# Talking-heads attention and gated layers on one core: score rows issued ahead of the stores of x in each slot

## The chip, the cores and the metric

One core of a Trainium2 chip. The metric is the device time of the kernel in microseconds (us), a median over runs; a profile of one execution by the hardware profiler goes with it.

## What is computed

```python
scores = (q @ k.T) / sqrt(64)                        # 4 batches, 12 heads, 448 x 448
scores = einsum('bhij,hg->bgij', scores, w_pre)      # heads mixed before the softmax
attn = softmax(scores)                               # exp(scores - max) / (sum + 1e-9)
attn = einsum('bhij,hg->bgij', attn, w_post)         # and after it
x = (attn @ v) as 1792 rows of 768
out = (sigmoid(x @ w_gate) * (x @ w_val)) @ w_out    # d_ff 1536
```

All inputs and the output are float32.

## The kernel before

The kernel has two stages in one program: the attention (`_attention`), which writes x to a buffer in device memory called xs, and the gated layers (`_Moe`), which read xs. The instruction order on every engine is fixed by the program's order; each engine works through its own queue, and semaphores hold an instruction until what it reads is there and what it overwrites has been read.

**Blocks and units.** Each batch has 448 query rows, cut into blocks of 120, 120, 120 and 88. A block is worked on in units: one or two sets of 10 query rows for all 12 heads. There are 16 blocks and 92 units (6, 6, 6 and 5 per batch; each batch's last unit has one set).

**Slots.** The loop that the diff touches (line 404 on) goes through slots `s`. In one slot several units are at different steps. The ones that matter here:

- `rows_until(s + LEAD, ...)` calls `regroup(s + 6)` (line 197): two transfers on SyncE's queue, one for each x in 0 and 1, that gather the score rows of unit s + 6 from the block's score tile `st` into a tile `T` with heads on the partitions. There are four `T` tiles, so the one for unit s + 6 is free when the premix of unit s + 2 has read it.
- `premix(s + 3)` (line 207): TensorE mixes the heads of unit s + 3, reading `T` half by half and writing `pm` banks. Three `pm` banks serve two sets a unit, so each premix needs a bank that the exponential of the unit before must have read.
- `rowmax` (line 215, VectorE), `expo` (line 225, ScalarE), `norm`, `scale` (GpSimd), `p_lo` (VectorE), `postmix` (line 255, TensorE), `mix` (line 263, ScalarE): the softmax and the second mixing.
- `scores` (line 159) and `keep` (line 165): scores of a later block, into `st`.
- `av` (line 273): attn @ v of a finished block, two pairs of heads at a time. After the fourth and the sixth pair ScalarE copies the result into the tile `xt` (line 292), and a store of `xt` to xs is put on the list `stores`. There is one `xt` tile (`xp` has one buffer), so the next copy into it must wait until the store before has landed. `av` stands in the last part of a slot.
- `flush()` (line 269) issues what is on the list, on SyncE's queue (line 271). The list also holds, twice, a small transfer of a bound (`max_x`).
- Last in a slot come loads on SyncE's queue: v (line 172), k (line 137), q (line 145) for the batches and blocks to come, and raw weights of the gated layers (line 1037).

So SyncE's queue gets, slot by slot: the stores that the slot before has put on the list, the rows of unit s + 6, then the slot's loads. Each block's two stores are flushed in the fourth and the sixth slot after that of the block's last unit, and with them go the rows of unit s + 6. From slot 83 on (`s >= NU - LEAD - 3`) the rows of the next slot are already issued inside the slot, so that the call at the top of the loop finds nothing to do.

```python
    def flush():
        while stores:
            nc.sync.dma_start(out=stores[0][0], in_=stores.pop(0)[1])
```

Of the kernel before, what the change touches and what calls it, by code (L numbers as in the profile page):

```python
# [41 lines left out]
def _attention(ctx, tc, ins, B, H, S, D, xs, raws, make_moe):  # L42
# [37 lines left out]
    def qk_banks():  # L80
        return [ps_qk.tile([128, 512], F32, tag="qk", name="qk") for _ in range(2)]
# [71 lines left out]
    def scores(bi, c, sc):  # L153
        b, n = blocks[bi][0], R * blocks[bi][4]
        q, k = q_t[bi], k_t[b, c]
        for s0, s1 in ((0, 64), (64, max(n, 100))):
            for e in range(2):
                rows = slice(64 * e, 64 * e + 64)
                nc.tensor.matmul(sc[e][s0:s1, :S], lhsT=q[c][rows, s0:s1], rhs=k[rows, :], start=True, stop=True)  # L159

    def keep(bi, c, e, sc):
        n = R * blocks[bi][4]
        if c == e == 0:
            st_t[bi] = stg[bi % ST].tile([QB, H, S], F32, tag="st", name="st")
        (nc.vector.tensor_copy if e else nc.scalar.copy)(st_t[bi][:n, 2 * c + e], sc[e][:n, :S])  # L165
# [31 lines left out]
    def regroup(u):  # L197
        bi, r0s, _, _, i = units[u]
        sets, st, T = blocks[bi][4], st_t[bi], t_bufs[u % len(t_bufs)]
        at = 64 - HK  # L200
        for x in range(2):
            if len(r0s) == 2:
                nc.sync.dma_start(out=T[at:at + 2 * HK, x], in_=st[i + x:sets * R:sets])
            else:
                nc.sync.dma_start(out=T[at:at + HK, x], in_=st[i + sets * HALF * x:sets * HALF * (x + 1):sets])

    def premix(u):
        T = t_bufs[u % len(t_bufs)]
        banks = units[u][2]
        for x in range(2):  # L210
            for i, bank in enumerate(banks):
                rows = slice(64, 64 + HK) if i else slice(0, 64)
                nc.tensor.matmul(pm[bank][64 * x:64 * x + 64, :S], lhsT=w1[rows], rhs=T[rows, x], start=True, stop=True)  # L213

    def rowmax(u):
        nm = sm.tile([128, 2], F32, tag="nm", name="nm")
        for i, bank in enumerate(units[u][2]):
            nc.vector.tensor_reduce(nm[:, i:i + 1], pm[bank][:, :S], axis=AX.X, op=ALU.max, negate=True)  # L218
        nm_t[u] = nm

    def expo(u, i):
        if i == 0:
            e_t[u] = ep.tile([128, 2, S], F32, tag="e", name="e")
            ss_t[u] = sm.tile([128, 2], F32, tag="ss", name="ss")
        nc.scalar.activation(out=e_t[u][:, i], in_=pm[units[u][2][i]][:, :S], func=AF.Exp, bias=nm_t[u][:, i:i + 1],  # L225
                             scale=1.0, accum_out=ss_t[u][:, i:i + 1])

    def norm(u):
        ss = ss_t[u][:, :len(units[u][1])]
        nc.gpsimd.tensor_scalar(ss, ss, 1e-9, 1.0 / P_UP, op0=ALU.add, op1=ALU.mult)  # L230
        nc.vector.reciprocal(ss, ss)  # L231

    def scale(u):

        ph = pp.tile([128, 2, S], F16, tag="ph", name="ph")
        for i in range(len(units[u][1])):
            nc.gpsimd.tensor_scalar(ph[:, i], e_t[u][:, i], ss_t[u][:, i:i + 1], 1.0, op0=ALU.mult, op1=ALU.mult)  # L237
        p_t[u] = [ph]

    def p_lo(u):  # L240
        pl = pp.tile([128, 2, S], F16, tag="pl", name="pl")
        for i in range(len(units[u][1])):
            nc.vector.scalar_tensor_tensor(pl[:, i], e_t[u][:, i], ss_t[u][:, i:i + 1], p_t[u][0][:, i],  # L243
                                           op0=ALU.mult, op1=ALU.subtract)
        p_t[u].append(pl)

    def postmix(u):
        mx = two_banks(ps_mx, "mx").rearrange("p x (i c) -> p x i c", i=2)[:, :, :, :4 * HK]
        ph, pl = p_t.pop(u)
        for i in range(len(units[u][1])):  # L250
            for jb in range(4):
                for k, (p, w) in enumerate(((ph, w2hi), (ph, w2lo), (pl, w2hi))):
                    for x in range(2):
                        rows = slice(64 * x, 64 * x + 64)
                        nc.tensor.matmul(mx[:, x, i, jb * HK:(jb + 1) * HK], lhsT=p[rows, i, JB[jb]:JB[jb] + 128], rhs=w[rows],  # L255
                                         start=(k == 0), stop=(k == 2))
        mx = mx.rearrange("p x i c -> p (x i) c") if len(units[u][1]) == 2 else mx[:, :, 0]
        mx_t[u] = mx.rearrange("p y (g r) -> p y g r", r=HALF)

    def mix(u):  # L260
        bi, r0s = units[u][:2]
        out = mixes[bi % 2].rearrange("p j h s -> p (j h) s")[:, :, r0s[0]:r0s[-1] + R]
        nc.scalar.activation(out=out.rearrange("p g (y r) -> p y g r", r=HALF), in_=mx_t.pop(u), func=AF.Copy,  # L263
                             scale=1.0 / (P_UP * W_UP))
# [4 lines left out]
# [3 lines that stand above are left out]
# [26 lines left out]
    LEAD = 6  # L298
# [12 lines left out]
    for b in range(B):  # L311
# [3 lines left out]
        s = f + 5  # L315
        for i in range(H // 2):
            s = max(s + 1, f + 6 + 2 * (2 * i // QUAD))
# [79 lines left out]
    def rows_until(u, done):  # L397
        while done < min(NU, u + 1):
            regroup(done)
            done += 1  # L400
        return done

    next_dma = 0
    for s in range(min(min(plan), -LEAD), max(plan) + 1):
        flush()
        next_dma = rows_until(s + LEAD, next_dma)
        todo = plan.get(s, ())
        jobs = [args for fn, args in todo if fn is scores]
        ahead_u = [(s + SOFT, i) for i in range(len(units[s + SOFT][1]))] if 0 <= s + SOFT < NU else []
        if 0 <= s + 1 < NU:  # L410
            norm(s + 1)
            scale(s + 1)
        if ahead_u:
            premix(s + SOFT)
            rowmax(s + SOFT)

        def job(bi, c):
            sc = qk_banks()
            scores(bi, c, sc)
            return lambda e: keep(bi, c, e, sc)  # L420

        kept = job(*jobs[0]) if jobs else None
        for i, e in enumerate(ahead_u[:1]):
            expo(*e)
        if kept:
            kept(0)
            kept(1)
        for c in hooks.get(s, ()):
            c.close()
        if 0 <= s + 1 < NU:  # L430
            p_lo(s + 1)
        tail = (av, moe.between, moe.early)
        if s == NU - 1:
            nc.scalar.activation(out=iw, in_=sw, func=AF.Sigmoid)
        if 0 <= s < NU:
            postmix(s)
        elif s >= NU:
            moe.slot(NG + s - NU)
        if 0 <= s < NU:
            mix(s)  # L440
        for e in ahead_u[1:]:
            expo(*e)
        for fn, args in todo:
            if fn is not scores and fn not in tail:
                fn(*args)
        if s >= NU - LEAD - 3:
            next_dma = rows_until(s + 1 + LEAD, next_dma)
        if 0 <= s < NU:
            for i in range(len(units[s][1])):
                moe.slot(units[s][3] + i)  # L450
        for fn, args in todo:
            if fn in tail:
                fn(*args)
        for args in jobs[1:]:
            kept = job(*args)
            kept(0)
            kept(1)
# [751 lines left out]
@with_exitstack  # L1209
def kernel(ctx, tc, B, H, S, D, ins, out):  # L1210
    nc = tc.nc
    top = ctx.enter_context(tc.tile_pool(name="top", bufs=1))
    dram = ctx.enter_context(tc.tile_pool(name="dram", bufs=1, space=DRAM))
    xs = dram.tile([B, H * D // 128, 128, S], F32, name="xs")
    with tc.manual_schedule():
        raws = top.tile([128, 13 * H * D // 2], F32, name="raws")
        with ExitStack() as c2:
            moe = _attention(c2, tc, ins, B, H, S, D, xs, raws,
                             lambda NG: _Moe(tc, xs, ins, out, raws, NG, top))
        moe.run()  # L1220
# [72 lines left out]
```

## Time and profile before

| what | value |
|---|---|
| median of 3 runs | 790.5 us (789.5 to 790.78) |
| the profiled execution | 792.71 us, of which the span of its instructions is 790.9 us |
| TensorE busy (PE) | 765.7 us, 97% of the span |
| VectorE (DVE), ScalarE (ACT), GpSimd (POOL) busy | 631.6, 566.5 and 256.0 us |
| granted TensorE clock, mean | 0.995 |
| DMA, mean | 210 GB/s |
| a pair of transfers of score rows T<-st | 2 x 210 KB |
| a store xs<-xt | 240 KB (four pairs of heads), 120 KB (two) |

The span runs from the first to the last instruction. Busy shares count an engine's own work, without its waits and without the issuing of DMAs. SyncE has no work of its own: it issues transfers, and an entry of its queue that waits holds all that stand behind it. In a row of the timeline, the time in brackets is what the engine stood idle before the instruction, and behind the arrow what ended that wait, as far as the profile infers it; where a wait has several causes, the one named is the one that came last by the profile.

### The profile page before, as it was taken

How to read it: one execution, taken by the hardware profiler on the slowest of the kernel's cores; microseconds unless marked ns; L12 is line 12 of the kernel's file. 1: busy time of each engine (PE TensorE's matmuls, PEld its weight loads, DVE VectorE, ACT ScalarE, POOL GpSimd, SP SyncE). 2: the span in 40 equal slices, each digit the busy share in tenths (PEclk: the TensorE clock that was granted, in tenths of full speed). 3: DMA queues.
4: the chain of work that ended last, by engine and by line, in shares of the span. 5: the costliest groups of instructions: out<-in, count | busy, mean ns of one | idle time of the engine just before them, and what ended most of it. 6: DMA issues, size and time to landing. Idle time of an engine off the chain costs nothing.

```text
span 790.9 us, 23630 instructions
## 1 busy us (share of the span) xinstructions
PE 765.7 (97%) x9626; PEld 422.9 (53%) x9626; DVE 631.6 (80%) x1092; ACT 566.5 (72%) x1122; POOL 256.0 (32%) x426
## 2 busy tenths in 40 slices
PE   8999999899989999978999999999999999999998
PEld 2465665566656666554555455555555555555554
DVE  4998899699969898889996988679786999997111
ACT  3899899798989899786975877677856784563000
POOL 1563547354644455420312222224322221010000
PEclk9999999999999999999999999999999999999999
DMA  5787678747885474828506384664567788995001
GB/s 193 248 241 222 205 247 259 241 165 234 269 257 186 172 239 158 279 82 283 183 6 221 107 271 159 264 221 148 208 190 264 275 310 298 386 363 206 36 36 70
DMA packets 80716, 166.16 MB, mean 210 GB/s; under 512 B 20448, under 2 KB 57664, under 8 KB 80608
## 3 DMA queue, kind: packets, MB, share of 16 engines
q1 hardware_dynamic: 72304, 132.88, 50.8%
q0 software_dynamic: 7728, 31.27, 10.2%
q8 instruction: 75, 1.23, 0.6%
q10 hardware_dynamic: 576, 0.51, 0.2%
q14 instruction: 33, 0.27, 0.1%
HBM read 87.77 MB, written 38.15 MB: 159 GB/s over the span
## 4 chain that ended last, share of the span: by engine, by line
PE 83%; DVE 6%; ACT 5%; DMA 3%; issue 2%; POOL 1%; SPq 0%; DVEq 0%; ACTq 0%; POOLq 0%
PE bank L1147 30%; PE bank L1158 18%; PE pm L213 10%; PE qk L159 9%; PE av L282 8%; PE mx L255 7%; DVE m L1131 2%; ACT e L225 1%; ACT m L1126 1%; ACT mix L263 1%; DVE pl L243 1%; DMA T<-st 1%; DVE m L1140 1%; DMA max_w<-junk 1%; DMA k<-in_kp_dram 1%
## 5 line engine op out<-in xcount | busy, mean ns | idle before, releaser
L1147 PEld LDWEIGHTS <-m 128*128 128x128 f16 x1512 | 147.5, 98 | 143.3 <-DVE m L1131 4.1
L1147 PE MATMUL bank<-m,m 128*128 128x448 f16 x1116 | 214.7, 352 | 4.3 <-DVE m L1131 3.2
L237 POOL TENSOR_SCALAR ph<-e,ss 128x448 f16<-128x448 f32 x180 | 112.6, 638 | 151.6 <-DVE ss L231 108.7
L225 ACT ACTIVATE e<-pm,nm 128x448 f32<-128x448 f32 x180 | 115.4, 641 | 30.6 <-DVE nm L218 28.2
L218 DVE TENSOR_REDUCE nm<-pm 128x1 f32<-128x448 f32 x180 | 103.4, 615 | 31.7 <-PE pm L213 28.4
L243 DVE SCALAR_TENSOR_TENSOR pl<-e,ss,ph 128x448 f16<-128x448 f32 x180 | 115.8, 683 | 2.0 <-POOL ph L237 2.0
L213 PE MATMUL pm<-T,w 64*64 64x448 f32 (+1 forms) x720 | 109.7, 563 | 4.1 <-ACT raws L1078 3.5
L1158 PEld LDWEIGHTS <-m 128*128 128x128 f16 x756 | 74.0, 98 | 69.0
L159 PE MATMUL qk<-k,q 64*64 64x448 f32 x736 | 103.4, 545 | 2.8 <-ACT st L165 2.0
L263 ACT ACTIVATE mix<-mx 128x960 f32<-128x960 f32 (+1 forms) x92 | 104.5, 1136 | 1.4 <-PE mx L255 1.4
L255 PEld LDWEIGHTS <-ph 64*128 64x128 f16 x2880 | 63.4, 93 | 71.7 <-issue 42.3
L1158 PE MATMUL bank<-m,m 128*128 128x448 f16 x468 | 92.9, 352 | 0.0
L282 PE MATMUL av<-mix,v 128*64 128x120 f32 (+1 forms) x1504 | 83.8, 264 | 0.2 <-issue 0.2
L255 PE MATMUL mx<-w2hi,ph 64*128 64x60 f16 x1440 | 71.1, 189 | 7.6 <-ACT mix L263 5.2
L1147 PE MATMUL bank<-m 128*128 128x448 f16 x396 | 77.9, 352 | 0.0
L282 PEld LDWEIGHTS av<-mix,v 128*64 128x64 f32 x1504 | 73.6, 138 | 3.0 <-issue 0.8
L255 PE MATMUL mx<-w2lo,ph 64*128 64x60 f16 x1440 | 70.3, 188 | 1.0 <-issue 1.0
L255 PE MATMUL mx<-w2hi,pl 64*128 64x60 f16 x1440 | 70.1, 188 | 0.5 <-DVE pl L243 0.5
L1084 POOL CAST raws<-raws 128x768 f16<-128x768 bf16 x28 | 31.4, 1122 | 118.1 <-ACT raws L1078 118.1
L1078 ACT ACTIVATE raws<-raws 128x768 int16<-128x768 int8 (+1 forms) x72 | 60.2, 836 | 11.3 <-POOL raws L1084 11.1
L165 DVE COPY st<-qk 120x448 f32<-120x448 f32 (+1 forms) x92 | 56.6, 615 | 8.7 <-PE qk L159 8.7
L255 PEld LDWEIGHTS <-pl 64*128 64x128 f16 x1440 | 61.3, 93 | 1.7 <-issue 1.1
(127 smaller groups left out, 1043.1 us busy)
## 6 DMA issues: line engine op xcount, KB each, us to landing
T<-st SPq DMA_DIRECT2D x176, 210.0 KB
m<-w SPq DMA_DIRECT2D x60, 384.0 KB
raws<-in_w_dram SPq DMA_DIRECT2D x28, 767.6 KB
hs<-m POOLq DMA_DIRECT2D x48, 224.0 KB, 3.1
m<-hs SPq DMA_DIRECT2D x15, 672.0 KB
w<-m POOLq DMA_DIRECT2D x21, 384.0 KB, 4.4
w<-raws POOLq DMA_DIRECT2D x20, 384.0 KB, 4.7
v<-in_vb_dram SPq DMA_DIRECT2D x12, 512.0 KB
```

The costliest lines, as they stand in the source:

```text
L159: nc.tensor.matmul(sc[e][s0:s1, :S], lhsT=q[c][rows, s0:s1], rhs=k[rows, :], start=True, stop=True)
L213: nc.tensor.matmul(pm[bank][64 * x:64 * x + 64, :S], lhsT=w1[rows], rhs=T[rows, x], start=True, stop=True)
L218: nc.vector.tensor_reduce(nm[:, i:i + 1], pm[bank][:, :S], axis=AX.X, op=ALU.max, negate=True)
L225: nc.scalar.activation(out=e_t[u][:, i], in_=pm[units[u][2][i]][:, :S], func=AF.Exp, bias=nm_t[u][:, i:i + 1], scale=1.0, accum_out=ss_t[u ...
L237: nc.gpsimd.tensor_scalar(ph[:, i], e_t[u][:, i], ss_t[u][:, i:i + 1], 1.0, op0=ALU.mult, op1=ALU.mult)
L243: nc.vector.scalar_tensor_tensor(pl[:, i], e_t[u][:, i], ss_t[u][:, i:i + 1], p_t[u][0][:, i], op0=ALU.mult, op1=ALU.subtract)
L255: nc.tensor.matmul(mx[:, x, i, jb * HK:(jb + 1) * HK], lhsT=p[rows, i, JB[jb]:JB[jb] + 128], rhs=w[rows], start=(k == 0), stop=(k == 2))
L263: nc.scalar.activation(out=out.rearrange("p g (y r) -> p y g r", r=HALF), in_=mx_t.pop(u), func=AF.Copy, scale=1.0 / (P_UP * W_UP))
L282: nc.tensor.matmul(av_t[bi][64 * i:64 * i + 64, c % 4, :n], lhsT=vt[b, u][:, h + i, jb, :], rhs=mixes[bi % 2][:, jb, 2 * c + i, :n], start ...
L1078: self.nc.scalar.activation(out=out, in_=src, func=AF.Copy, scale=by)
L1147: self.nc.tensor.matmul(self.f32(bank), lhsT=w[a][:, k], rhs=x[b][:, k], start=self.START[i] and k == r == 0, stop=k == self.KH - 1 and r ...
L1158: self.nc.tensor.matmul(self.f32(bank), lhsT=w[a][:, k], rhs=b[bb], start=self.START[i] and j == k == r == 0, stop=j == OUT_TILES - 1 and ...
```

## The change

In each slot, the transfers of score rows are issued first and the stores on the list behind them; before it was the other way round.

```diff
--- before.py
+++ after.py
@@ -402,8 +402,8 @@
 
     next_dma = 0
     for s in range(min(min(plan), -LEAD), max(plan) + 1):
+        next_dma = rows_until(s + LEAD, next_dma)
         flush()
-        next_dma = rows_until(s + LEAD, next_dma)
         todo = plan.get(s, ())
         jobs = [args for fn, args in todo if fn is scores]
         ahead_u = [(s + SOFT, i) for i in range(len(units[s + SOFT][1]))] if 0 <= s + SOFT < NU else []
```

The instructions on TensorE, VectorE, ScalarE and GpSimd keep their order; only SyncE's queue differs. First place: SyncE at slot 9, the first store of the first block (`xs<-xt`), the rows of unit 15 (tile `T_173`, two transfers) and the loads around them. Before:

```order
L145 DMA q<-in_qp_dram 128x720
L1037 DMA raws<-in_w_dram 128x1536
L271 DMA xs<-xt 128x4x120
L203 DMA T_173<-st 120x1x448 x2
L137 DMA k<-in_kp_dram 128x448
L1037 DMA raws<-in_w_dram 128x1533
```

and with the change:

```order
L145 DMA q<-in_qp_dram 128x720
L1037 DMA raws<-in_w_dram 128x1536
L203 DMA T_173<-st 120x1x448 x2
L271 DMA xs<-xt 128x4x120
L137 DMA k<-in_kp_dram 128x448
L1037 DMA raws<-in_w_dram 128x1533
```

The store has moved behind the pair of rows; the load of k that follows is the same. The first stores of the blocks in slots 32 and 55 stand in the same way behind the rows of units 38 and 61.

Second place: SyncE at slots 26 to 29, where the loads of batch 2 begin. Before:

```order
L271 DMA xs<-xt 128x4x88
L203 DMA T_170<-st 120x1x448 x2
L203 DMA T_171<-st 120x1x448 x2
L172 DMA v<-in_vb_dram 128x1024
L271 DMA xs<-xt 128x2x88
L203 DMA T_172<-st 120x1x448 x2
L1037 DMA raws<-in_w_dram 128x1536
L203 DMA T_173<-st 120x1x448 x2
L172 DMA v<-in_vb_dram 128x1024
L137 DMA k<-in_kp_dram 128x448 x2
```

and with the change:

```order
L203 DMA T_170<-st 120x1x448 x2
L271 DMA xs<-xt 128x4x88
L203 DMA T_171<-st 120x1x448 x2
L172 DMA v<-in_vb_dram 128x1024
L203 DMA T_172<-st 120x1x448 x2
L271 DMA xs<-xt 128x2x88
L1037 DMA raws<-in_w_dram 128x1536
L203 DMA T_173<-st 120x1x448 x2
L172 DMA v<-in_vb_dram 128x1024
L137 DMA k<-in_kp_dram 128x448 x2
```

The raw weights, and the loads of v and k after them, now stand directly behind the store, and no longer behind the store and a pair of rows. In all, 26 stores of x move in this way.

## Rows read from the trace of the kernel before

**Rows 1.** The page, section 4: the chain that ended last, by engine.

```profile
PE 83%; DVE 6%; ACT 5%; DMA 3%; issue 2%; POOL 1%; SPq 0%; DVEq 0%; ACTq 0%; POOLq 0%
```

**Rows 2.** Windows: us, busy time (instructions) by engine, granted clock, DMA share, GB/s.

```profile
50.00:62.00 12.00, 12.00 (x307) 7.93 (x305) 9.93 (x21) 12.00 (x33) 7.95 (x12) 1.00 0.90 251
...
122.00:146.00 24.00, 21.44 (x476) 12.72 (x469) 19.74 (x42) 19.31 (x47) 15.08 (x21) 1.00 0.84 261
...
182.00:204.00 22.00, 22.00 (x502) 13.65 (x504) 21.02 (x53) 20.51 (x51) 10.32 (x21) 1.00 0.80 248
204.00:230.00 26.00, 23.99 (x543) 14.72 (x539) 22.52 (x48) 22.87 (x57) 17.68 (x24) 0.99 0.89 268
...
17.00:340.00 323.00, 311.67 (x7030) 187.54 (x7024) 282.21 (x605) 285.69 (x666) 161.30 (x280) 0.99 0.71 226
...
228.60:232.00 3.40, 3.40 (x16) 1.37 (x16) 0.92 (x4) 3.13 (x8) 1.44 (x3) 0.66 0.71 235
232.00:236.00 4.00, 4.00 (x92) 2.73 (x92) 2.68 (x6) 3.43 (x8) 0.00 (x0) 0.86 0.68 228
```

**Rows 3.** Waits on SyncE's queue: us in total, times, longest.

```profile
SPq L271 <- ACT xt L292: 65.1, 26, 10.6
```

**Rows 4.** Tile T: issues (ns min/median/max); waits ended by its landing (us, times).

```profile
L203 SPq DMA_DIRECT2D T<-st x176: 760/768/1335, 12.0 to 319.5; - x176
...
  DMA T<-st: 1.7, 4
```

**Rows 5.** Timeline of SyncE, slot 9: start, us, line, operation [idle before].

```profile
54.71 0.57 SPq L271 DMA_DIRECT2D xs<-xt  x1
```

**Rows 6.** Timeline of all engines, 60 to 70 us.

```profile
61.00 0.51 ACT L292 ACTIVATE xt<-av,sw 128x240 f32<-128x240 f32 x1
...
62.81 0.20 PEld L213 LDWEIGHTS pm<-T,w 64*64 64x64 f32 x4 [0.45 <-DMA T<-st]
...
68.74 0.22 PEld L159 LDWEIGHTS qk<-k,q 64*64 64x64 f32 x8 [0.77 <-ACT st L165]
...
69.55 0.64 ACT L225 ACTIVATE e<-pm,nm 128x448 f32<-128x448 f32 x1 [0.86 <-DVE nm L218]
```

**Rows 7.** Timeline of SyncE, 117 to 140 us.

```profile
120.18 0.38 SPq L271 DMA_DIRECT2D xs<-xt  x1
120.66 1.68 SPq L203 DMA_DIRECT2D T<-st  x2
122.42 0.45 SPq L1037 DMA_DIRECT2D raws<-in_w_dram  x1
...
137.09 0.38 SPq L271 DMA_DIRECT2D xs<-xt  x1
```

**Rows 8.** Timelines of ScalarE and TensorE's weight loads, 134 to 147 us.

```profile
136.16 0.14 PEld L213 LDWEIGHTS pm<-T,w 64*64 64x64 f32 x2 [0.75 <-DMA T<-st]
...
144.79 0.46 ACT L292 ACTIVATE xt<-av,sw 128x240 f32<-128x240 f32 x1 [3.56 <-DMA xs<-xt]
...
145.75 0.19 PEld L213 LDWEIGHTS pm<-T,w 64*64 64x64 f32 x2 [2.49 <-ACT raws L1078]
146.35 0.28 PEld L213 LDWEIGHTS pm<-T,w 60*64 60x64 f32 x6 [0.41 <-ACT e L225]
```

**Rows 9.** Timelines of SyncE, ScalarE and TensorE's weight loads, 219 to 231 us.

```profile
219.71 0.38 SPq L271 DMA_DIRECT2D xs<-xt  x1
...
222.11 1.63 PEld L282 LDWEIGHTS av<-mix,v 128*64 128x64 f32 x32
...
227.60 0.46 ACT L292 ACTIVATE xt<-av,sw 128x240 f32<-128x240 f32 x1 [1.79 <-PE mx L255]
...
228.57 0.19 PEld L213 LDWEIGHTS pm<-T,w 64*64 64x64 f32 x2 [1.14 <-ACT raws L1078]
229.16 0.19 PEld L213 LDWEIGHTS pm<-T,w 60*64 60x64 f32 x2 [0.40 <-ACT e L225]
229.65 0.29 PEld L213 LDWEIGHTS pm<-T,w 64*64 64x64 f32 x4 [0.30 <-DMA T<-st]
```

## The prediction

> **What bounds the kernel now.** I read the page first. The chain that ended last is TensorE for 83% [rows 1], so a transfer matters only where TensorE waits for it, directly or through another engine. The diff changes the order on SyncE's queue and nothing else, and only in the attention, so the second view is the busy time by stretch: from 17 to 340 us TensorE is busy 311.67 of 323.00 us [rows 2]. At most 11.3 us are to be had there, and whatever is added to its waits lasts to the end, because the gating layers begin from the x that the attention stores.
>
> Third come SyncE's own waits. In 26 places the store of x stands at the head of the queue until ScalarE has written xt, 65.1 us in all [rows 3]; the transfers of score rows, behind it, stand with it. Against that, TensorE waited for rows of T only four times, 1.7 us together, and one transfer of rows takes SyncE 0.768 us to issue [rows 4], a pair 1.68 [rows 7]. The obvious gain of the change, rows that come earlier, is therefore worth at most 1.7 us. The reader should keep this: the queue is held for long, but what it holds has slack.
>
> The timeline shows where there is no slack. The key and query loads of the next batch fall in three stretches, and in each the first store of a block is followed at once by a unit's rows.
>
> - **Slot 9** (A): store 54.71, its rows next. ScalarE writes the next xt at 61.00 without having waited; TensorE gets the second half of those rows at 62.81 [rows 5, 6].
> - **Slot 32** (B): store 137.09, its rows next in the queue [rows 7]. ScalarE stands still for 3.56 us until 144.79, when that store has landed (there is one xt tile, so the next copy into it waits for the store before): 7.7 us from issue to landing. TensorE stands for 2.49 us until 145.75 [rows 8].
> - **Slot 55** (C): store 219.71, its rows next. ScalarE stands until 227.60. The row names a postmix matmul, but xt reads av, whose weights were loaded from 222.11 on for 1.63 us; so it was the store again, 7.9 us after its issue. TensorE takes the first rows at 228.57, waits for ScalarE's exponentials at 229.16 and for the second rows at 229.65 [rows 9].
>
> The DMA engines are 0.90, 0.84 and 0.89 busy in these stretches, against 0.71 over the attention [rows 2].
>
> **The change, part by part.** No instruction is added or removed.
>
> *The push.* A store now lies behind two transfers of rows. Where the queue is backlogged, it should land about when those rows landed before. C: 229.65 − 227.60 = 2.05 us later. B: the last rows come into use in the weight loads at 146.35, so 146.35 − 144.79 = 1.56, say 1.6. A: 62.81 − 61.00 = 1.8, if the store landed just before 61.00. No row shows that landing; but successive transfers land 1.08 us apart at C (228.57 and 229.65), and 62.81 less twice that is 60.7, so I take nearly all of it, 1.75. The lower bound is 0 at A, and 0 at B and C if the DMA engines do not keep the order of issue.
>
> What hangs on it: ScalarE's xt copy, and behind it on ScalarE the exponential of the next unit, for which TensorE's premix needs its bank.
>
> - A: ScalarE shows no idle time from 61.00 until 69.55, and at 68.74 TensorE waits 0.77 us for a copy out of that train [rows 6]. So the whole delay reaches TensorE: **+1.75**.
> - B: premix's wait for ScalarE and its last rows fall into one row, 146.35, so TensorE loses about what ScalarE loses: **+1.6** before the next item.
> - C: the wait for ScalarE moves from 229.16 to 231.2 against 229.65 for the rows: +1.55, or +2.05 counted on ScalarE.
>
> *The lead.* The rows no longer stand behind the store that waits, so what follows the store is issued earlier by a pair's time: the raw weights at 122.42 could follow the store of 120.18 at about 120.66, 1.76 us earlier [rows 7], and the loads of batch 2 behind them likewise. Where the DMA engines had time free before, that lead is kept until B. I take 1.35 of 1.76, because the next unit's rows also need scores that are copied only in that slot: B is **+0.25**. Before A there is no earlier store, hence no lead. Before C the engines were already 0.80 busy from 182 to 204 [rows 2], where a transfer issued earlier mostly queues longer; I take 0.7, between 0 and 1.4. C then costs ScalarE 1.35 and TensorE 0.75 to 1.35: **+1.05**.
>
> *Rows earlier.* At 136.16 TensorE waited 0.75 us for rows [rows 8]. The lead takes that wait away; late next is ScalarE's exponential, which the same step needs, so I count **−0.5** (between 0 and −0.75). The waits for rows at A and C are inside the terms above.
>
> *The other 23 of the 26 stores that move.* Rows now go out while SyncE waits for xt, and 65.1/26 = 2.5 us of waiting covers the 1.68 of issuing. The next copy into xt is far: 6.3 us lie between the store at 54.71 and the copy at 61.00, even at A. I cost these stores nothing; where the cover is missing, one costs up to 1.7 us.
>
> Sum: 1.75 + 0.25 + 1.05 − 0.5 = **+2.55 us** on the profiled execution of 792.71 (a span of 790.9 and 1.8 around it), which stands 0.28% over the median of 790.5. Carried to the median: **793.0**, 0.3% slower.
>
> *The clock.* After its wait at C, TensorE was granted 0.66 of its clock from 228.6 to 232 and 0.86 from 232 to 236 [rows 2]: part of that time it ran at 1.2 GHz. That is 0.34 × 3.4 + 0.14 × 4 = 1.7 us of full clock, the most that such a drop costs. One drop more or less is not in the sum, but in the range.
>
> **A rule to weigh.** The row shows 7.7 us from issue to landing at B. The Trainium skill, "DMA: Bandwidth & Descriptors", section "Anatomy of one DMA — SWDGE (gpsimd) path", gives a fixed 2 us plus bytes over 436 GB/s; by that a 240 KB store takes 2.55 us (an estimate from the page), lands well before ScalarE needs xt, and the sum would be −0.5, no change. The trace disagrees threefold and has the duration itself, so I leave that outcome 0.03 of the chance for no change.
>
> **The rivals.**
>
> 1. *The lead pays for the push* (no change). If the whole 1.76 is kept at C too, C costs 2.05 − 1.76 = 0.3, the sum is 1.75 + 0 + 0.3 − 0.5 = 1.55, and if a shorter wait at C also spares the clock drop, −0.15. Middle +0.7: 791.2. For it: from 182 to 204 the engines were 0.80 busy, not full, so there is room for earlier work. Against: A has no lead at all.
> 2. *No lead* (slower). The engines are so full that early issue only queues: 1.75 + 1.6 + 1.55 = +4.9: 795.4. Against it: between the store at 120.18 and the raw weights at 122.42 SyncE did nothing but issue (0.38 and 1.68 of the 2.24 us), so it held the engines back there, not they it.
> 3. *The push does not happen* (faster). It decides whether a store issued behind rows lands behind them. If the transfers share the engines instead, the stores land no later, and with the lead of 1.76 at B and 1.0 at C both stalls of ScalarE shrink: −1.6 − 1.0 − 0.5 (rows at 136.16) − 0.45 (rows at 62.81) = −3.55: 787.0. For it: TensorE's idle 2.49 us at B is there to be won. Against: at C store, first rows and second rows came home in their order of issue, 227.60, 228.57, 229.65.
>
> That the change does nothing is not likely: SyncE's order differs at all these stores.
>
> **How the numbers follow.** A measurement of this kernel tells 0.2%, 1.6 us, from no change. Forecast, 0.38, own range 792.3 (C's whole lead of 1.4) to 794.7 (one clock drop more); no lead, 0.12: both slower, 0.50. Lead pays, 0.33: same. No push, 0.17: faster. The range runs from 789.3, a third of the way from no change to the faster case (−3.55/3 = −1.2), to 795.8, the no-lead case and 0.4 for the sizes in it; some 0.18 lies outside.
>
> **What would show it.** In the new profile, ScalarE should idle about 1.7 us before its second xt copy near 61 us, with TensorE's wait for ScalarE right after; the wait before the copy near 145 should stay near 3.6 us; the one near 228 should grow by 1 to 2 us; the wait for rows near 136 should vanish, and SyncE's waits at the store should fall well below 65 us. The forecast is wrong if ScalarE does not wait at A, or if the stalls at B and C shrink.

## The result, and the profile after

| | median us | runs | ratio to before |
|---|---|---|---|
| before | 790.78 | 11 | |
| the change | 797.66 | 11 | 1.0078 (95% interval 1.0055 to 1.0101) |

The change is slower by 0.78%, some 6.2 us, where 793.0 was forecast in a range of 789.3 to 795.8: the right side, but well over twice the +2.55. The profiled execution of the change took 798.64 us, with a span of 796.9 against 790.9.

I read the new profile in the order of the prediction. First the page's chain that ended last, which answers to [rows 1]:

```profile
PE 80%; ACT 6%; DMA 5%; DVE 5%; POOL 2%; issue 1%; SPq 1%; ACTq 0%; DVEq 0%; POOLq 0%
```

TensorE has lost 3 points, ScalarE and the DMA engines have won 1 and 2. Next, busy time by stretch (us, busy time and instructions of PE, PEld, DVE, ACT and POOL, granted clock, DMA share, GB/s). The changed kernel:

```profile
17.00:340.00 323.00, 312.84 (x6951) 187.01 (x6944) 277.15 (x598) 282.28 (x659) 157.57 (x277) 0.98 0.69 223
...
64.00:70.00 6.00, 5.28 (x88) 3.37 (x90) 2.97 (x5) 6.00 (x15) 1.44 (x3) 0.72 0.70 236
122.00:146.00 24.00, 24.00 (x549) 14.36 (x546) 21.70 (x47) 21.27 (x52) 16.79 (x22) 1.00 0.84 273
...
125.41:149.41 24.00, 22.81 (x513) 13.32 (x506) 20.72 (x44) 21.51 (x53) 16.60 (x21) 1.00 0.83 270
...
232.00:240.00 8.00, 5.86 (x79) 3.54 (x80) 3.67 (x8) 6.53 (x15) 1.44 (x3) 0.57 0.55 185
```

and the kernel before, in the first and the last of these places:

```profile
64.00:70.00 6.00, 6.00 (x132) 3.39 (x130) 4.55 (x10) 5.14 (x14) 2.25 (x5) 1.00 0.76 257
228.00:236.00 8.00, 7.40 (x104) 4.13 (x108) 3.67 (x8) 7.16 (x18) 1.44 (x3) 0.79 0.69 231
```

From 17 to 340 us TensorE is as busy as before, 312.84 us against 311.67 [rows 2], but it has come less far, 6951 matmuls against 7030: its granted clock is 0.98 where it was 0.99, so for a larger part of that time it ran at 1.2 GHz. From 64 to 70 us the granted clock is 0.72 where it was 1.00, and from 232 to 240 it is 0.57, where one such stretch of 8 us had 0.79. From 122 to 146 us TensorE seems to do better than before, 24.00 us busy and 21.44 then [rows 2]. But the changed kernel comes to this place 3.41 us later (ScalarE's ninth copy into xt starts at 136.81, it was 133.40), and its wait, 1.96 us until 147.46, lies outside this window. The window moved by 3.41 us has 22.81 us busy, 1.4 more than before.

The waits on SyncE's queue (us in total, times, longest), which answer to [rows 3]. The changed kernel:

```profile
SPq L271 <- ACT xt L292: 41.6, 18, 11.2
SPq L203 <- PE qk L159: 36.5, 40, 2.8
SPq L203 <- PE pm L213: 27.9, 37, 2.7
SPq L203 <- PE mx L255: 25.9, 41, 1.0
SPq L203 <- DVE st L165: 21.2, 10, 7.2
```

The kernel before, the same waits at the rows:

```profile
SPq L203 <- PE mx L255: 24.2, 44, 0.8
SPq L203 <- PE pm L213: 24.1, 40, 1.0
SPq L203 <- PE qk L159: 19.3, 29, 1.9
SPq L203 <- DVE st L165: 13.5, 5, 6.8
```

The waits at the store fell from 65.1 to 41.6 us, but those four waits at the rows rose from 81.1 to 111.5 (sums of the rows). The queue is held as long as before; the head of it is now more often a transfer of rows.

Now the three places. SyncE's queue at A (slot 9) and C (slot 55):

```profile
54.50 2.24 SPq L203 DMA_DIRECT2D T<-st  x2
56.85 0.43 SPq L271 DMA_DIRECT2D xs<-xt  x1
...
221.37 0.33 SPq L145 DMA_DIRECT2D q<-in_qp_dram  x1
222.78 1.81 SPq L203 DMA_DIRECT2D T<-st  x2
224.68 0.44 SPq L271 DMA_DIRECT2D xs<-xt  x1
```

ScalarE's second copy into xt at A, B and C, which answer to 61.00 [rows 6], 144.79 [rows 8] and 227.60 [rows 9]:

```profile
63.59 0.46 ACT L292 ACTIVATE xt<-av,sw 128x240 f32<-128x240 f32 x1 [2.07 <-DMA xs<-xt]
...
145.90 0.46 ACT L292 ACTIVATE xt<-av,sw 128x240 f32<-128x240 f32 x1 [1.45 <-DMA xs<-xt]
...
232.66 0.46 ACT L292 ACTIVATE xt<-av,sw 128x240 f32<-128x240 f32 x1 [4.83 <-DMA xs<-xt]
```

and TensorE's weight loads for the premix behind each of them:

```profile
64.72 0.20 PEld L213 LDWEIGHTS pm<-T,w 60*64 60x64 f32 x6 [2.16 <-ACT e L225]
...
147.46 0.20 PEld L213 LDWEIGHTS pm<-T,w 60*64 60x64 f32 x6 [1.96 <-ACT e L225]
...
234.22 0.30 PEld L213 LDWEIGHTS pm<-T,w 60*64 60x64 f32 x6 [2.91 <-ACT e L225]
```

The chain is the one that was forecast: the store is issued behind the rows, it lands later, ScalarE's next copy into the only xt tile waits for it, the exponential behind that copy is late, and TensorE's premix stands for its bank. At A the store went out at 56.85 and not at 54.71 [rows 5], and ScalarE, which had not waited there before, waits 2.07 us. From issue to the copy that it lets go are 63.59 − 56.85 = 6.7 us. (By the fixed 2 us and 436 GB/s of the Trainium skill, "DMA: Bandwidth & Descriptors", section "Anatomy of one DMA — SWDGE (gpsimd) path", the estimate was 2.55 us; the trace disagrees here too. It agrees elsewhere: in the same profile the stores of this size issued at 79.5 and 250.4 us landed after 2.41 and 2.43 us, with the DMA engines 0.61 and 0.57 busy there.) At C the copy that fills xt ended at 219.79, and the store was issued 4.9 us later; before, it was 1.3 us (218.39 to 219.71). At B ScalarE's wait is shorter than before, 1.45 against 3.56.

### The profile page after: what moved, and what is told of

The parts are those of the page before. It is cut to its first block, busy times and chain, and to the rows that moved or that the text cites. A ratio compares the mean times of both kernels' runs of the same rounds, so it can differ in the third digit from the quotient of the medians.

```text
span 796.9 us, 23624 instructions
## 1 busy us (share of the span) xinstructions
PE 770.0 (97%) x9626; PEld 425.7 (53%) x9626; DVE 631.9 (79%) x1092; ACT 566.9 (71%) x1122; POOL 253.6 (32%) x426
## 3 DMA queue, kind: packets, MB, share of 16 engines
q0 software_dynamic: 7728, 31.27, 10.2%
## 4 chain that ended last, share of the span: by engine, by line
PE 80%; ACT 6%; DMA 5%; DVE 5%; POOL 2%; issue 1%; SPq 1%; ACTq 0%; DVEq 0%; POOLq 0%
PE bank L1147 32%; PE bank L1158 18%; PE pm L213 9%; PE qk L159 8%; PE av L282 7%; PE mx L255 6%; ACT e L225 2%; DVE m L1131 2%; ACT mix L263 2%; DMA T<-st 2%; DMA m<-xs 1%; DMA xs<-xt 1%; DVE pl L243 1%; DVE nm L218 1%; ACT st L165 1%
## 5 line engine op out<-in xcount | busy, mean ns | idle before, releaser
L282 PE MATMUL av<-mix,v 128*64 128x120 f32 (+1 forms) x1504 | 86.0, 269 | 0.0
L282 PEld LDWEIGHTS av<-mix,v 128*64 128x64 f32 x1504 | 76.0, 141 | 2.7 <-issue 0.4
L1078 ACT ACTIVATE raws<-raws 128x768 int16<-128x768 int8 (+1 forms) x72 | 60.1, 835 | 10.8 <-POOL raws L1084 10.6
L1174 DVE TENSOR_TENSOR m<-bank,m 128x448 f32<-128x448 f32 x72 | 44.5, 620 | 23.8 <-PE bank L1147 15.6
```

What stands on the lines that cost most here:

```text
L282: nc.tensor.matmul(av_t[bi][64 * i:64 * i + 64, c % 4, :n], lhsT=vt[b, u][:, h + i, jb, :], rhs=mixes[bi % 2][:, jb, 2 * c + i, :n], start ...
```

## The experiments

Single executions scatter, so two measures are used for every run. One is the median with its ratio to before. The other is the profile's own: the time from the start of ScalarE's first copy into xt to the start of the third (**stretch A**, slots 9 to 13), from the ninth to the eleventh (**B**, slots 32 to 36) and from the seventeenth to the nineteenth (**C**, slots 55 to 59), read from the starts of these copies in each trace.

### One part of the change at a time

Each is the kernel before with the rows first only in the slots named:

```diff
+        if s == 9:
+            next_dma = rows_until(s + LEAD, next_dma)
         flush()
         next_dma = rows_until(s + LEAD, next_dma)
```

The other conditions are `s == 55`, `24 <= s <= 32`, `47 <= s <= 55` and `s not in (9, 55)`. Expected:

> The change in slot 9 alone. Theory 1: ScalarE waits about 2 us before its copy near 63 us, TensorE stands 1.4 us and then runs at half rate for one stretch of some 3.4 us (1.7 us lost): 3 us slower than before, 793 to 794. Rival (the delay at slot 9 is taken up by the slack before slot 32, where ScalarE waits anyway): the shift is gone by 150 us and the time is that of before within 0.2%.

> The change in slot 55 alone. Theory 1 (the push costs at slot 55 by itself): ScalarE's wait near 228 us grows from 1.79 to 3 to 5 us; 1.5 to 3.1 us for TensorE and up to 1.7 us more by a longer half-rate stretch, 792.5 to 795. What the runs so far give by difference: the change against the change without slots 9 and 55 is 5.8 us, slot 9 alone 1.1 (against the same runs of before), so slot 55 about 4 us. Rival (slot 55 loses only after earlier slots have moved too, because their loads then lie in its way): within 0.2% of before.

> The change in slots 24 to 32 alone: the stores at slots 26 and 28 move behind their rows, so that the loads of batch 2 can leave earlier, and so does the store at slot 32. Theory 1 (the lead is worth more than the push at slot 32, as the profile of the change showed: ScalarE's wait there 1.45 us where it was 3.56): 2 us faster than before, 789 to 790. Rival A (the forecast's own term): +0.25 for the push against -0.5 for the rows, the same within 0.2%. Rival B (what the profile of the change showed at slot 32 came from its delay of 3 us at slot 9, since the loads had that much longer to land): no gain, or 1.6 us slower.

> The change in slots 47 to 55: the stores of the block before, at slots 49 and 51, move behind their rows too, so that the loads of the next batch can leave earlier. Theory 1 with the lead that was forecast (0.7 us at slot 55): about 0.7 us better than slot 55 alone. Rival (no lead at slot 55, since what leaves earlier only queues longer): the same as slot 55 alone or slower, ScalarE's wait near 228 us 4 us or more.

> The change in every slot except 9 and 55, where the store stays ahead of the rows. Theory 1 (slots 9 and 55 lose, slot 32 gains by loads that leave earlier): slot 9 and 55 as before, slot 32 about 2.4 us better, 788 to 789, faster than before by 0.2 to 0.3%. Rival (the loss is made in many slots, and 9 and 55 are only where it shows): 794 or more.

| rows first in | median us | ratio (95%) | A | B | C |
|---|---|---|---|---|---|
| slot 9 | 792.79 | 1.0027 (1.0004 to 1.0050) | 22.67 | 23.35 | 27.29 |
| slot 55 | 795.25 | 1.0036 (1.0015 to 1.0058) | 21.33 | 24.07 | 26.56 |
| slots 24 to 32 | 794.40 | 1.0036 (1.0012 to 1.0059) | 21.24 | 24.96 | 24.97 |
| slots 47 to 55 | 797.16 | 1.0051 (1.0029 to 1.0074) | 21.56 | 25.74 | 29.40 |
| all but 9 and 55 | 791.84 | 1.0004 (0.9977 to 1.0031) | 21.20 | 26.09 | 25.27 |

Slot 9 alone costs 0.27%, slot 55 alone 0.36%; without these two the other slots cost nothing that can be told from 0. That fits theory 1 on where the loss is made. The gain that it expected at slot 32 (788 to 789 us) did not come. Two results bear on the forecast of a lead. With slots 47 to 55 moved, so that the loads before C can leave earlier, ScalarE's wait at C is longer than with slot 55 alone, where it was 2.46 us:

```profile
229.81 0.46 ACT L292 ACTIVATE xt<-av,sw 128x240 f32<-128x240 f32 x1 [3.96 <-DMA xs<-xt]
```

This is one profile of each, and the same order has waits of 1.29 to 4.83 us there in six profiles of the change (below). The timed runs, 0.51% and 0.36%, show no gain by a lead, but their intervals overlap. And with slots 24 to 32 moved the kernel is slower, not faster as I had read from the first pair of profiles. SyncE's queue shows what became of the lead there; the first key loads, the query load, the store and its rows, in slots 24 to 32 moved:

```profile
124.67 1.04 SPq L137 DMA_DIRECT2D k<-in_kp_dram  x2
...
134.76 0.43 SPq L145 DMA_DIRECT2D q<-in_qp_dram  x1
135.99 0.78 SPq L1039 DMA_DIRECT2D raws<-in_w_dram  x1
136.88 1.67 SPq L203 DMA_DIRECT2D T<-st  x2
138.94 0.68 SPq L271 DMA_DIRECT2D xs<-xt  x1
```

and in the kernel before:

```profile
125.25 1.12 SPq L137 DMA_DIRECT2D k<-in_kp_dram  x2
...
134.55 0.33 SPq L145 DMA_DIRECT2D q<-in_qp_dram  x1
136.13 0.33 SPq L1037 DMA_DIRECT2D raws<-in_w_dram  x1
```

The moved kernel stood 0.66 us later as a whole when it came here (its third copy into xt starts at 75.97, that of before at 75.31). With 0.66 taken off, the key loads leave 1.24 us earlier, the query load only 0.45. In time, the lead is nearly used up within ten microseconds, because here an issue waits for a landing (last section). Against the engines it is not: this kernel has lost another 2.0 us between the third and the ninth copy (60.12 against 58.09), at waits of TensorE whose cause the profile does not name, so that the query load leaves 2.0 us before the end of the ninth copy (136.77), where in the kernel before it left 0.5 us after it (134.06). That profile is of a run of 791.25 us, the second fastest of its 12. So what a typical run of these slots loses is not shown; and all slots but 9 and 55, which include these, cost 0.04%. If the others among them neither gain nor lose, the two intervals leave 0.12 to 0.31%.

### A second xt tile

The last two pairs of heads get a tile of their own, so that no copy has to wait for the store just before it. I ran it with both orders, and with rows first up to slot 40 only:

```diff
             elif bi == NBK - 2 and c0:
...
+            elif c0 and bi < NBK - 3:
+                xt = kst.tile([128, 2, QB], F32, tag="xt2", name="xt2", bufs=1)[:, :, :n]
             else:
...
+        if s <= 40:
+            next_dma = rows_until(s + LEAD, next_dma)
         flush()
```

(the last three lines only in the third kernel, `two_xt_rows_first_to_40`).

> The order of before, but the copy of the last two pairs of heads goes to a tile of its own, so that no copy of ScalarE has to wait for the store of the four pairs in front of it. Theory 1 (ScalarE's wait for a store is what TensorE stands still for at slots 32 and 55): ScalarE's idle times before the copies near 145 and 228 us (3.56 and 1.79 us before) are gone, with them TensorE's idle 2.49 us near 146 and about 1 us near 229, and perhaps the clock drop near 230 (1.7 us): 3 to 5 us faster than before, 786 to 788. Rival (rows are what TensorE waits for there, ScalarE's wait only lies beside it): the waits move to the rows, within 1 us of before.

> The order of the change, with the same second tile. Theory 1 (the store behind the rows lands later, and only ScalarE's next copy into the one xt tile suffers): ScalarE's waits near 63, 145 and 232 us are gone (2.07, 1.45 and 4.83 us with the change), TensorE's half-rate stretches near 66 and 233 us too, and the time is that of the order of before with two tiles, within 0.2%: 786 to 788, some 10 us below the change with one tile. Rival A (TensorE's half-rate stretches come of themselves with this order, or from later loads and not from the copy): it stays over 793. Rival B (the change also brings rows too late somewhere else): 2 us or more above the order of before with two tiles.

> A second xt tile for the last two pairs, rows first up to slot 40 and stores first after it. By the drifts of the two profiles with two tiles (rows first stands at -3.9 us from slot 40 to 58, stores first loses nothing more behind it and gains 2.4 at slot 62): 786 to 789, the fastest so far. Rival (one profile's drift is a matter of chance, both two-tile kernels have medians within 1.4 us of before): 789.5 to 791.5.

> A second xt tile for the last two pairs, rows first up to slot 40, stores first behind it, timed again: if its gain is real, 0.1 to 0.4% faster than before (it was 0.25%, interval 0.07 to 0.43%), and about 0.7% faster than the change on the same chip. If it was chance, within 0.1% of before.

| second xt tile | median us | ratio to before (95%) | A | B | C |
|---|---|---|---|---|---|
| stores first | 790.61 | 0.9982 (0.9962 to 1.0003) | 21.33 | 23.79 | 24.15 |
| rows first | 791.11 | 1.0000 (0.9977 to 1.0023) | 21.26 | 22.42 | 26.71 |
| rows first to slot 40 | 789.29 | 0.9975 (0.9957 to 0.9993) | 21.24 | 22.48 | 25.55 |
| the same again | 789.89 | 0.9987 (0.9959 to 1.0015) | 21.25 | 22.43 | 24.55 |

This is the test of the cause. With the second tile the order of the change has the ratio 1.0000 where it was 1.0078; against the order of before, also with two tiles, that is 0.18% more, which the intervals do not tell from 0. ScalarE's second copy at A does not wait, though the store goes out at 56.80, as late as in the change:

```profile
61.40 0.55 ACT L294 ACTIVATE xt<-av,sw 128x240 f32<-128x240 f32 x1
```

So the loss, or at least most of it, needs the single xt tile. But neither order gets the 786 to 788 us that I expected. At C with rows first TensorE stands 2.02 us before an av matmul, and no releaser is named; ScalarE's copy of that result then waits:

```profile
239.65 1.31 PE L282 MATMUL av<-mix,v 128*64 128x120 f32 x11 [2.02 <-issue]
...
241.00 0.66 ACT L294 ACTIVATE xt<-av,sw 128x480 f32<-128x480 f32 x1 [1.70 <-PE av L282]
```

Mixing the two orders was the fastest kernel, 0.25% under before in one timing and 0.13% in the other, where the interval takes in 1: faster than the change for certain, faster than before by about 0.2%, if at all.

### Stores from ScalarE's own queue

```diff
     def flush():
         while stores:
-            nc.sync.dma_start(out=stores[0][0], in_=stores.pop(0)[1])
+            nc.scalar.dma_start(out=stores[0][0], in_=stores.pop(0)[1])
```

> Before, but the stores of x are issued from ScalarE's own queue, right behind the copy that writes xt, so that neither the rows stand behind a store that waits, nor a store behind SyncE's backlog. One xt tile. If issue order on SyncE is what delays the stores at slots 32 and 55 (3.03 and 1.32 us between the end of the copy and the issue), the waits before the copies near 145 and 228 us shrink by that much and TensorE gains 2 to 4 us: 787 to 789; an issue takes ScalarE about 0.45 us (its queue's rows at the start of the trace), 26 to 34 of them, of which most lies in idle time. Rival (the DMA engines are full there, and the order of issue only decides who waits): the wait moves to the rows or to loads of k and v, and the time is that of before within 0.3%, or worse by ScalarE's issue time.

> Both together: a second xt tile, and stores issued from ScalarE's queue. If waits for the store are all there is to win at slots 9, 32 and 55: no more than with two tiles alone, 789 to 791. If SyncE's held queue costs something beside: 1 to 2 us below that. Rival (DMA engines full): same as two tiles alone within 0.2%, with waits for rows, k or v in the place of the store.

Measured: 805.11 us, ratio 1.0162 (1.0129 to 1.0195), and with two tiles 806.15, 1.0169 (1.0133 to 1.0204). Both theories were far off. ScalarE at slot 9, one xt tile:

```profile
55.30 0.66 ACT L292 ACTIVATE xt<-av,sw 128x480 f32<-128x480 f32 x1
57.97 0.40 ACTq L271 DMA_DIRECT2D xs<-xt  x1
58.47 0.63 ACT L225 ACTIVATE e<-pm,nm 128x448 f32<-128x448 f32 x1 [2.51 <-DMA k<-in_kp_dram]
```

The copy ended at 55.96 and the store needs nothing else, but its issue waits until 57.97 for a load of k to land, and the exponential stands behind it. The wait that SyncE had, which costs nothing there, is now on an engine that TensorE waits for: stretch A is 25.39 us in place of 21.30. This accounts for 4.1 of the 14 us between the two profiles (spans of 805.2 and 790.9); the cause of the rest (another 5 between the eleventh and the seventeenth copy) is not shown.

### Six profiles of the change, three of before

> The change once more, for a second profile. If the waits are the order's own: ScalarE waits about 2 us before its copy near 63 us and 4 to 5 us before the one near 232, with half-rate stretches of TensorE behind both; if they were chance, they differ by more than 1 us.

> The kernel before once more, for a second profile. If the waits are the order's own: no wait of ScalarE before the copy near 61 us, about 3.6 us before the one near 145 and 1.8 before the one near 228. If slot 32 varies from run to run, the wait near 145 differs by more than 1 us.

> A third profile of the change. If the waits are what a typical run loses: ScalarE waits 1 us or more before its copy near 63 us, 2 us or more before the one near 230, and TensorE's half-rate stretches follow them. If the loss is elsewhere: waits as in the kernel before (none near 61, 1.8 near 228), and half-rate stretches that begin without a wait.

> A fourth profile of the change, with the same expectations as the third: waits near 63 and 230 us, or waits as before.

> A fifth profile of the change, with the same expectations as the third: waits near 63 and 230 us, or waits as before.

> A third profile of the kernel before. It tells how far its own waits scatter: 3.56 and 2.47 us near 145, 1.79 and 1.75 near 228 in the first two; if the third lies in the same bounds, a wait of over 2.5 us near 228 belongs to the change.

> The change, timed again, with a sixth profile. If the loss is the waits at slots 9 and 55 with the half-rate stretches behind them (1.5 and 2.2 us on the mean of the profiles), it is 3 to 4.5 us, 0.4 to 0.6% over before. If the first timing holds (0.55 to 1.0%), something that the profiles do not show is lost beside them.

ScalarE's second copies at A, B and C in the second profile of the change:

```profile
61.77 0.53 ACT L292 ACTIVATE xt<-av,sw 128x240 f32<-128x240 f32 x1
...
143.50 0.46 ACT L292 ACTIVATE xt<-av,sw 128x240 f32<-128x240 f32 x1 [1.73 <-DMA xs<-xt]
...
226.64 0.46 ACT L292 ACTIVATE xt<-av,sw 128x240 f32<-128x240 f32 x1 [2.12 <-DMA xs<-xt]
```

and in the second profile of before:

```profile
143.61 0.46 ACT L292 ACTIVATE xt<-av,sw 128x240 f32<-128x240 f32 x1 [2.47 <-DMA xs<-xt]
...
227.04 0.46 ACT L292 ACTIVATE xt<-av,sw 128x240 f32<-128x240 f32 x1 [1.75 <-DMA xs<-xt]
```

All nine, with ScalarE's wait before its second copy and the stretch (11 to 17: from the eleventh copy to the seventeenth; 29 to 31: the last copies of the attention):

| profile | us | A: wait, stretch | B: wait, stretch | 11 to 17 | C: wait, stretch | 29 to 31 | span |
|---|---|---|---|---|---|---|---|
| before | 792.71 | 0, 21.30 | 3.56, 26.35 | 57.97 | 1.79, 26.51 | 12.06 | 790.9 |
| before, 2nd | 792.34 | 0, 21.20 | 2.47, 25.63 | 58.07 | 1.75, 26.20 | 13.32 | 790.6 |
| before, 3rd | 790.46 | 0, 21.23 | 2.26, 26.00 | 58.09 | 1.87, 24.94 | 11.59 | 788.7 |
| change | 798.64 | 2.07, 24.39 | 1.45, 23.98 | 58.34 | 4.83, 30.54 | 13.31 | 796.9 |
| change, 2nd | 793.74 | 0, 21.22 | 1.73, 24.26 | 58.02 | 2.12, 26.34 | 14.44 | 792.0 |
| change, 3rd | 794.75 | 2.01, 23.35 | 1.94, 24.46 | 58.05 | 3.95, 28.03 | 12.07 | 793.0 |
| change, 4th | 791.55 | 0.48, 21.81 | 2.12, 25.42 | 58.19 | 2.64, 25.89 | 11.56 | 789.8 |
| change, 5th | 799.38 | 1.88, 23.22 | 1.75, 25.09 | 58.99 | 3.85, 29.63 | 13.32 | 797.6 |
| change, 6th | 797.81 | 1.90, 23.24 | 2.73, 25.21 | 61.89 | 1.29, 25.55 | 13.31 | 796.0 |
| mean of change less mean of before | | +1.63 | −1.26 | +0.87 | +1.78 | +0.68 | +4.15 |

The five columns are +3.7 of the +4.15; the rest, +0.5, lies before the first copy, where the queue still has the order of before, so it is scatter. The waits belong to the order, but not to every run: A waits 1.9 to 2.1 us in four of six, C 3.85 to 4.83 in three of six. The expectation that an execution either shows them all or none fails. In the sixth the loss is a new one: TensorE stands 2.21 us until 214.38 in a premix, and behind it its granted clock is 0.50 from 214.7 to 218.1. The profile names no cause; the rows that this premix reads, issued from 200.48 on, had landed by 208.9:

```profile
214.38 0.20 PEld L213 LDWEIGHTS pm<-T,w 64*64 64x64 f32 x7 [2.21 <-issue]
```

The sixth run also timed the change again in five rounds: 797.77 us, ratio 1.0082 (1.0055 to 1.0110), where the profiles had made me expect 0.4 to 0.6%. So the 0.8% is firm. That the nine profiles show 2 us less can be chance: the spans of the six alone go from 789.8 to 797.6 us, and the difference of the two means has a standard error of 1.4 us.

What an execution loses at C can be taken apart. The granted clock over stretch C is 1.00, about 0.94 or about 0.88; three profiles of the change, the fourth, the third and the fifth:

```profile
218.21:244.10 25.89, 23.09 (x500) 13.32 (x496) 20.05 (x42) 22.09 (x55) 10.76 (x19) 1.00 0.76 247
...
219.25:247.28 28.03, 24.68 (x492) 13.78 (x488) 20.05 (x43) 22.26 (x56) 10.07 (x19) 0.94 0.73 232
...
220.60:250.23 29.63, 26.12 (x500) 15.16 (x504) 20.05 (x43) 22.39 (x54) 10.50 (x19) 0.88 0.68 217
```

The waits in the runs of parts of the change are 2.65 us (slot 9), 2.46 (slot 55), 2.04 (24 to 32), 3.96 (47 to 55) and 2.06 (all but 9 and 55). With ScalarE's wait taken off the stretch, the 14 profiles with one xt tile fall into three groups:

| granted clock over stretch C | at 1.2 GHz | profiles | stretch less wait |
|---|---|---|---|
| 1.00 | none | before 3rd, change 4th, slots 24 to 32, all but 9 and 55 | 22.93 to 23.25, mean 23.1 |
| 0.93 to 0.94 | 3.4 us | before 1st and 2nd, change 2nd, 3rd and 6th, slot 9, slot 55 | 24.08 to 24.72, mean 24.4 |
| 0.88 to 0.89 | 6.8 us | change 1st and 5th, slots 47 to 55 | 25.44 to 25.78, mean 25.6 |

So stretch C is 23.1 us, plus ScalarE's wait, plus 1.2 to 1.3 us for each 3.4 us at 1.2 GHz.

## Why the prediction was right or wrong

**The bound, and what rows first could win.** Right. The wait for rows near 136 us is gone (the weight loads at 138.13 in the new profile begin without one), SyncE's waits at the store fell by a third, and nothing came of either. What I did not see is that the rows then wait at the head of the queue in the store's place.

**A, +1.75.** Right in mechanism and size: ScalarE waits 2.07 us and TensorE 2.16, the stretch costs 1.63 on the mean, slot 9 alone 0.27% (2.1 us, interval 0.04 to 0.50%). The guess that the store had landed just before 61.00 was right too: the trace has it at 60.75.

**B, +0.25, with −0.5 for rows.** Not decided. The wait near 145, which I said would stay near 3.6, was 1.45; but the 3.56 of the first profile was the largest of nine. The order of before at slot 32 (three profiles of before, and the runs of slot 9, 55, and 47 to 55) gives a mean stretch of 25.2, the order of the change (six profiles, slots 24 to 32, all but 9 and 55) 24.9: −0.3, against the −0.25 of the two terms. The timed run of slots 24 to 32 says +0.36%, which these stretches do not show.

**C, +1.05.** Mis-sized: it came to +1.9 us, and in the timed run of slot 55 alone to 0.36% (2.9 us, interval 0.15 to 0.58%). In the first profile ScalarE's wait grew by 3.0 us, but that profile is the extreme. Over all profiles with one tile, the wait is 2.0 us on the mean in the six with the order of before at slot 55 and 3.1 in the eight with that of the change: +1.1, near the 1.35 that the push less the lead gave ScalarE. (The 0.75 for TensorE should be 1.55 − 0.7 = 0.85, which changes little.) The stretch grew by more, from 25.86 to 27.74. The rest, 0.8 us, goes with time at 1.2 GHz: 1.7 us of it on the mean in the six, 4.3 in the eight.

**The lead, "I take 0.7, between 0 and 1.4".** Not decided. In the first profile there was none: the query load left 1.6 us after the end of the copy that fills xt, 0.1 us in the kernel before. On the mean over the seven profiles in which slots before 55 moved too, the store landed 10.8 us after the end of that copy, and 9.5 us in the six with the order of before: +1.4, as the 1.35 has it. But with slot 55 alone, where no lead is possible, it landed after 9.8 us, so this does not show a lead. The prediction's argument that SyncE held the engines back, "not they it", was read from the pair of issues at 120.18 and 122.42; at 134.55, in the same profile, the query load waited for a landing.

**The clock, "not in the sum".** This is the step that failed: the sum put the slower clock behind a longer wait at nothing and left it to the range. After some of these waits TensorE runs at 1.2 GHz, for 3.4 us or twice that: at A after one wait of four, at B in four profiles of nine, at C in seven of nine (twice for 6.8 us, as from 232.8 to 239.7 in the first profile of the change, against 229.7 to 233.1 in the first of before). What 3.4 us of it cost is 1.2 to 1.3 us at C (table above); at A the stretch is 24.39 us with and 23.22 to 23.35 without, 1.0 to 1.2. Up to the end of the attention the profiles have 6.8, 17.1 and 10.2 us of it before, and 20.5, 17.1, 6.8, 10.2, 20.5 and 17.1 with the change: 4.0 us more on the mean, an estimated 1.5 us of time. But 2.3 of the 4.0 lie from 334 us on, where it is not shown that the change has a part in it. The timed executions point the same way: their mean granted clock is 0.9891 in the 17 of the change and 0.9928 in the 98 of the kernel before that were timed beside the experiments, which is 17.3 and 11.3 us at 1.2 GHz. Those 6 us more are worth 2.2 of the 6.2 us, an estimate by the price at C. A forecast can't say which wait brings it, but it can put a mean price on each.

**What the sum then misses.** In the profiles A, B and C together came to 1.63 − 1.26 + 1.78 = 2.15 us, near the 2.55. The other 2 us lie where the prediction expected nothing: 0.87 between the eleventh and the seventeenth copy, nearly all of it from the fifth and the sixth profile of the change, 0.68 at the end of the attention, and 0.5 before the first copy, which is scatter. The timed runs put the loss at slots 9 and 55 (0.27 and 0.36%) and nothing that they can tell in the rest (0.04%).

**The rivals.** "No lead", 795.4 at a chance of 0.12, came nearest in its number, but by luck: its loss of 1.6 us at B did not come, and it lacks the clock. "No push" is excluded by the wait at A and by the second tile; "the lead pays", no change, by the timed 0.8%.

**What stays open:** whether the timed 6.2 us and the profiles' 4.15 differ by more than chance, what part of the lead is kept at C, why the clock falls after one wait and not after another, and what slots 24 to 32 cost.

## What to carry to other kernels

A transfer that is moved back in a queue can land later (counted from the end of the copy that it stores, by 2.4 us at A and 3.7 at C in the first profiles), and the price is paid by whoever needs its buffer next: ask for each of them how many buffers it has, and give the tile a second one before reordering its queue. Waits at the head of a queue that cost nothing there can be passed on to an engine that everything waits for, as stores issued from ScalarE showed (+1.6%). And a sum built on one profile inherits its chance: the wait of 3.56 us on which a term rested was 0.84 to 2.5 us in five other executions of the same order.

## What the runs showed of the hardware

- **Issues are held by landings.** In these traces the transfers that SyncE issues use eight semaphores in turn, and an issue begins only when the transfer eight before it has landed. In the profile of the change, 11 of the 14 issues from 216.49 to 230.04 us begin 0.02 to 0.07 us after such a landing (the store at 224.68 had 0.4 us to spare, its rows at 222.78 none). In the profile of before 18 of the 319 issues up to 345 us begin within 0.08 us of such a landing, and 15 of these lie at A, B and C. So an earlier place in the queue need not be an earlier issue there. Stores that ScalarE issues take their turn at the same eight semaphores; that is why ScalarE waited for a load of k, which was the transfer eight before.
- **The same transfer takes 2.4 us more in one run than in another.** The store of slot 9, issued at 56.85 and 56.71 us in the first two profiles of the change, landed after 6.65 us in one and after 4.26 in the other. In the first the copy waited until 63.59; in the second the copy at 61.77 had not waited at all.
- **The same wait brings a clock drop in one execution and none in another.** TensorE waited 2.16 us at A in the first profile of the change and 2.12 in the third. In the first the granted clock then was 0.72 from 64 to 70 us; in the third it stayed at its higher level:

```profile
64.00:72.00 8.00, 6.17 (x111) 3.37 (x110) 4.83 (x11) 7.56 (x18) 1.72 (x4) 1.00 0.76 249
```
